# Left-over block before the last whole block, and one norm set for batches 2 and 3, in a cross-covariance attention and channel-mix kernel

## Chip, cores and metric

The kernel runs on one core of a Trainium2 chip. The metric is device time in microseconds (us); the time before is the median of 8 executions. A profile is of one execution. TensorE is PE in its rows (PEld are its weight loads), VectorE is DVE, ScalarE is ACT, GpSimd is POOL, and SyncE is SP.

## What is computed

There are four batches of N = 6208 tokens with C = 256 channels. Channel attention makes x, and a channel mix with a token shift makes the output:

```python
qn = q / (np.linalg.norm(q, axis=1, keepdims=True) + 1e-06)   # norms over the tokens
kn = k / (np.linalg.norm(k, axis=1, keepdims=True) + 1e-06)
a = softmax(kn.transpose(0, 2, 1) @ qn / tau)                 # 256 x 256 per batch
x = v @ a
xk = mu_k * x + (1 - mu_k) * x_prev                           # x_prev: one token earlier
xr = mu_r * x + (1 - mu_r) * x_prev
k = np.maximum(xk @ w_k, 0.0)                                 # 256 -> 1024
out = sigmoid(xr @ w_r) * (k * k @ w_v)                       # 1024 -> 256
```

tau is 1. Inputs and output are float32; the matmuls work on bfloat16.

## The kernel before

**Blocks.** Each batch's tokens are cut into 12 blocks of 512 and 64 left over. The left-over tokens of the four batches make one further block of 256 tokens, called "left". There are 49 blocks; "left" stands last (`blocks`, `LAST`). A block has subtiles of 128 tokens: four, and two in "left".

**One loop sets the order.** Nothing is scheduled by a tool: the loop over i (block) and j (eight steps), from line 606, records the instructions of every engine in the order in which that engine runs them. T = 8i + j counts the steps. In one pass i the work of several blocks is interleaved:
- `up(i+1, j)` (lines 334, 338): two matmuls of 512 columns into a bank kT_ps (three of them), then a relu on ACT into kr. `square(i+1, ..)` (line 345) squares a pair of these on DVE into kk. The four pairs are recorded at steps 2, 4 and 6 and at step 0 of the next pass: that last one is the last square.
- `gate_mm(i, s)` (line 355): the gate's matmuls into g_ps, and `gate_act` (line 390) a tanh on ACT into res.
- `down(i, j)` (line 384): kk times w_v into v_ps, three and five matmuls of 256 columns for each subtile. `finish` (line 397) multiplies on DVE by the gate and sends the block's 512 KB to memory from SP (line 400).
- `x_half(i+2, ..)` (lines 260, 262): x of a later block, two matmuls and a copy on ACT. `mix_delta` and `mix` (lines 302, 313, and 305, 318 for "left"): xk and xr on DVE. xk of block i+2 is made at steps 4 to 6 and is needed by `up(i+2, 0)` at the start of the next pass.

**The next batch's attention runs beside this.** The rows of q and k of batches 1 to 3 come in 13 groups for each batch: the 64 left-over rows first, then 12 groups of 512 rows (`GORD`). `unit(b, g, s)` takes 128 rows: two matmuls into s_ps (line 424) and one squaring on ACT (line 428) into sq. `due` spreads the units of a batch over 12 passes. sq tiles share a ring of eight buffers (`f4`) with res.

**Norms.** The squares have to be summed over all rows. `take_sum` adds sq tiles on DVE: a first add (line 456) makes acc, further adds (line 459) add to it, and a merge (line 463) makes a 128 x 512 tile t1; the left-over rows are only cast to it (line 465). `take_norm` multiplies t1 by a column of ones on PE: four matmuls of one column into n_ps (line 476), a norm set, copied by ACT (line 478) into a column of ssq. In batches 2 and 3 three groups share one acc (`MERGE = 3`), which gives five sets for a batch with that of the left-over rows; batch 1 has a set for each group. After a batch's last set comes its softmax chain (`softmax_pieces`): ten small pieces at ten steps, mostly on DVE.

**When a sum runs.** `sums` is a queue; `unit` appends to it, and the loop takes one entry at a step by

```python
            if j in (2, 3, 6, 7) or len(sums) > 2:
                take_sum()
```

**The end.** The last pass has only the down-projection of "left". `down` gives each of its two subtiles a bank of its own (line 370), multiplies it by the gate (line 373), and sends its rows in pieces of 64 KB, half on SP's queue and half on ACT's (line 378). The banks v_ps are two and go round.

Of the kernel before, what the change touches and what calls it, by code (L numbers as in the profile page):

```python
# [10 lines left out]
F32 = mybir.dt.float32  # L11
# [3 lines left out]
OP = mybir.AluOpType  # L15
# [3 lines left out]
def kernel(  # L19
# [13 lines left out]
    nc = tc.nc  # L33
    B, N, C = q.shape
    D = C
    DF = moe_w_k.shape[1]
    P = 128
    M = 512
    S = M // P
    assert C == 256 and DF == 1024  # L40
    NB = N // M
    L = N - NB * M
# [11 lines left out]
    ps = ctx.enter_context(tc.tile_pool(name="ps", bufs=1, space=bass.MemoryType.PSUM))  # L54
# [36 lines left out]
    NPE = 4  # L91
# [121 lines left out]
                pn.tile([P, 2], F32, name="sm"), pn.tile([P, 2], F32, name="mx"))  # L213


    blocks = [(b, t) for b in range(B) for t in range(NB)] + ["left"]
    NBLK = len(blocks)
    LAST = NBLK - 1
    LR = L + 16
    xl = const.tile([P, 2, B, L + 1], BF16, name="xl")  # L220
    st = {}

    def size(i):
        return M if i < LAST else B * L

    def v_load(i):
        b, t = blocks[i]
# [67 lines left out]
    def mix_delta(i):  # L295
        delta = p2.tile([P, 2, M], BF16, name="delta", tag="delta", bufs=2)
        st[i, "d"] = delta
        st[i, "xk"] = p2.tile([P, 2, M], BF16, name="xk", tag="xk", bufs=3)
        st[i, "xr"] = p2.tile([P, 2, M], BF16, name="xr", tag="xr", bufs=3)
        if i < LAST:  # L300
            o = blocks[i][1] * M
            nc.vector.tensor_tensor(delta, X[:, :, o + 1:o + 1 + M], X[:, :, o:o + M], op=OP.subtract)  # L302
        else:
            for dh in range(2):
                nc.vector.tensor_tensor(delta[:, dh, :B * L].rearrange("p (b l) -> p b l", b=B),
                                        xl[:, dh, :, 1:], xl[:, dh, :, :L], op=OP.subtract)

    def mix(i, key, dh):
        mu = mu_k_t if key == "xk" else mu_r_t
        o = st[i, key]  # L310
        if i < LAST:
            c = blocks[i][1] * M
            nc.vector.scalar_tensor_tensor(o[:, dh], st[i, "d"][:, dh], mu[:, dh:dh + 1],  # L313
                                           X[:, dh, c:c + M], op0=OP.mult, op1=OP.add)
        else:
            def r(a):
                return a.rearrange("p (b l) -> p b l", b=B)
            nc.vector.scalar_tensor_tensor(r(o[:, dh, :B * L]), r(st[i, "d"][:, dh, :B * L]), mu[:, dh:dh + 1],
                                           xl[:, dh, :, :L], op0=OP.mult, op1=OP.add)
# [27 lines left out]
    def gate_mm(i, s):  # L347
        if s * P >= size(i):
            return
        if s % 2 == 0:  # L350
            st[i, "g", s // 2] = ps.tile([P, 2, D], F32, name="g_ps", tag="g")
        g_ps = st[i, "g", s // 2]
        xr = st[i, "xr"]
        for dh in range(2):
            nc.tensor.matmul(g_ps[:, s % 2], xr[:, dh, s * P:(s + 1) * P], w_r_sb[:, dh, :],  # L355
                             start=s % 2 == 0 and dh == 0, stop=dh == 1, skip_group_check=True)

    def down(i, j):
        s, h = divmod(j, 2)
        if s * P >= size(i):  # L360
            return
        kk = st[i, "kk"]
        if (i, "res") not in st:
            st[i, "res"] = pq.tile([P, S, D], F32, name="res", tag="f4", bufs=NF)
        if i == LAST:
            if h == 0:
                st[i, "v1", s] = ps.tile([P, 2, D], F32, name="v_ps", tag="v", bufs=2)
            v_ps = st[i, "v1", s][:, 0]
            for fh in (range(3) if h == 0 else range(3, 8)):
                nc.tensor.matmul(v_ps, kk[:, fh, s * P:(s + 1) * P], w_v_sb[:, fh, :], start=fh == 0, stop=fh == 7)  # L370
            if h == 1:
                res = st[i, "res"]
                nc.vector.scalar_tensor_tensor(res[:, s], res[:, s], 1.0, v_ps, op0=OP.add, op1=OP.mult)  # L373
                for b in range(B):
                    u, o = divmod(b * L, P)
                    if u == s:
                        eng = nc.sync if o == 0 else nc.scalar
                        eng.dma_start(out[b, NB * M:, :], res[o:o + L, s, :])
            return
        if j % 4 == 0:  # L380
            st[i, "v", s // 2] = ps.tile([P, 2, D], F32, name="v_ps", tag="v", bufs=2)
        v_ps = st[i, "v", s // 2]
        for fh in (range(3) if h == 0 else range(3, 8)):
            nc.tensor.matmul(v_ps[:, s % 2], kk[:, fh, s * P:(s + 1) * P], w_v_sb[:, fh, :],  # L384
                             start=s % 2 == 0 and fh == 0, stop=fh == 7, skip_group_check=True)

    def gate_act(i, u):

        if (i, "g", u) in st:
            nc.scalar.activation(st[i, "res"][:, 2 * u:2 * u + 2], st.pop((i, "g", u)), AF.Tanh, scale=0.5)  # L390

    def finish(i, u):
        if (i, "v", u) not in st:
            return
        res = st[i, "res"]
        r = res[:, 2 * u:2 * u + 2]
        nc.vector.scalar_tensor_tensor(r, r, 1.0, st.pop((i, "v", u)), op0=OP.add, op1=OP.mult)  # L397
        if u == 1:
            b, t = blocks[i]
            nc.sync.dma_start(out[b, t * M:(t + 1) * M, :].rearrange("(s p) c -> p s c", p=P), res)  # L400

# [4 lines left out]
    sums = []  # L406
# [8 lines left out]
    def unit(b, g, s):  # L415
        rows, n = rows_of(g)
        if g == GORD[0] and s == 0:
            cov[b] = ps.tile([P, 2, C], F32, name="s_ps", tag="s")
            ssq[b] = pn.tile([P, 4, NB + 1], F32, name="ssq")
            ncol[b] = 0  # L420
        G = groups[b, g]
        qk = G["qk"]
        for ih in range(2):
            nc.tensor.matmul(cov[b][:, ih, :], qk[:rows, s, 1, ih * P:(ih + 1) * P], qk[:rows, s, 0, :],  # L424
                             start=g == GORD[0] and s == 0 and ih == 0, stop=g == GORD[-1], skip_group_check=True)
        if s % 2 == 0:
            G["sq", s // 2] = pq.tile([P, 2, 2, C], F32, name="sq", tag="f4", bufs=NF)
        nc.scalar.activation(G["sq", s // 2][:rows, s % 2], qk[:rows, s], AF.Square)  # L428
        if s == n - 1:
            if n == S:  # L430
                m = (GORD.index(g) - 1) % MERGE if b > 1 else 0
                if m == 0:
                    sums.append((b, g, 1))
                else:
                    sums.append((b, g, 3))
                    sums.append((b, g, 4))
                if b == 1 or m == MERGE - 1:
                    sums.append((b, g, 2))
            else:
                sums.append((b, g, 0))  # L440

    sums = []
    norms = []
    acc = {}

    MERGE = 3

    def take_sum():
        if not sums:
            return  # L450
        b, g, w = sums.pop(0)
        rows, n = rows_of(g)
        G = groups[b, g]
        if w == 1:
            acc[b] = pq.tile([P, 2, 2, C], F32, name="acc", tag="acc", bufs=2)
            nc.vector.tensor_tensor(acc[b], G["sq", 0], G["sq", 1], op=OP.add)
            return
        if w > 2:
            nc.vector.tensor_tensor(acc[b], acc[b], G["sq", w - 3], op=OP.add)  # L459
            return  # L460
        t1 = pq.tile([P, 2, C], BF16, name="t1", tag="t1", bufs=4)
        if w == 2:
            nc.vector.tensor_tensor(t1, acc[b][:, 0], acc[b][:, 1], op=OP.add)
        else:
            nc.vector.tensor_copy(t1[:rows], G["sq", 0][:rows, 0])
        norms.append((b, g, t1, T + 2))
# [139 lines left out]
    for i in range(-2, NBLK):  # L606
        for j in range(8):
            T = i * 8 + j
            if i == LAST - 1 and j == 7:

                st[LAST, "res"] = pq.tile([P, S, D], F32, name="res", tag="f4", bufs=NF)
                for s in range(2):
                    gate_mm(LAST, s)
                gate_act(LAST, 0)
            if j in (2, 6):
                gate_act(i, j // 4)
            if 0 <= i + 1 < NBLK:
                up(i + 1, j)
# [12 lines left out]
            n = i + 2  # L631
            if n == 0 and j == 0:
                x_first()
            if 0 < n < LAST:
                if j == 0:
                    x_half(n, 0)
                if j == 2:
                    x_half(n, 1)
# [10 lines left out]
                mix(i + 1, "xr", j)  # L649
            if j == 7 and 2 <= i + 3 < NPE:  # L650
                v_transpose_pe(i + 3, st.pop((i + 3, "v")), 0, S, "s")
            if j == 1 and NPE <= i + 5 < LAST:
                v_transpose_dma(i + 5)
            if j == 2 and NPE < i + 7 < LAST:
                v_load(i + 7)
            bank_x = i >= 0 and i % NB == 6 and j == 4
            if chain and (chain[0] is None or chain[0].__name__ != "bcast" or j in (4, 6)):
# [3 lines left out]
                    bank_x = f.__name__ == "bcast"  # L661
            if j in (4, 6) and not bank_x or j in (3, 5) and len(norms) > 1:
                take_norm()
            if j in (2, 3, 6, 7) or len(sums) > 2:
                take_sum()
            for u in due.get(T, []):
                b, g, s = units[u]
# [48 lines left out]
```

## Time and profile before

| | |
|---|---|
| median of 8 runs | 512.21 us (511.02 to 514.38) |
| the profiled execution | 513.14 us, of it the span 511.4 us |
| mean granted TensorE clock | 0.994 |
| last DVE instruction | starts at 506.96 us, takes 0.42 us |
| sums of batches 2 and 3 | about 140 to 370 us |

A row of the timeline has start, duration, engine, line, operation, output <- inputs, shape, and how many instructions it merges; in square brackets stands the idle time before it and what ended it. Durations of matmuls include the passage through the array, so that rows of back-to-back matmuls overlap: the distance of their starts is what one of them costs.

### The profile page before, as it was taken

The numbers are of one execution on the slowest core, as the hardware profiler recorded it, in microseconds if no ns is written. First come the engines' busy times: TensorE is split into PE (matmuls) and PEld (weight loads), VectorE is DVE, ScalarE is ACT, GpSimd is POOL, SyncE is SP. The second block draws the span as 40 slices with busy tenths as digits, with TensorE's granted clock in tenths as the row PEclk, the third lists the DMA queues.
The fourth block names the chain that finished last, engine by engine and source line by source line (L and its number), as shares of the span: only waits on it lengthen the run. The fifth ranks groups of instructions, "written<-read, shape, count | busy, mean of one in ns | idle before, by whom it ended". The sixth has DMA issues, their size and how long they took to land. (4 is left out here: it accounts for less than half of the span.)

```text
span 511.4 us, 9779 instructions
## 1 busy us (share of the span) xinstructions
PE 494.0 (97%) x3720; PEld 339.4 (66%) x3720; DVE 445.1 (87%) x704; ACT 432.4 (85%) x817; POOL 106.2 (21%) x145
## 2 busy tenths in 40 slices
PE   5799999999999999999999999999999999999996
PEld 2474677776676677677666767767666666666675
DVE  3467799999999999999999999999998787878884
ACT  6787999999999898898998899899787877787773
POOL 0036523422431231221342132100121100000000
PEclk9999999999999999999999999999999999999999
DMA  8999999999999999999699999952299674332213
GB/s 313 396 304 190 195 190 197 195 218 195 171 194 181 167 174 165 174 166 162 111 185 196 189 181 157 151 128 72 62 152 163 104 144 114 76 105 61 75 50 104
DMA packets 143343, 83.48 MB, mean 163 GB/s; under 512 B 51200, under 2 KB 139840, under 8 KB 143296
## 3 DMA queue, kind: packets, MB, share of 16 engines
q0 software_dynamic: 65808, 33.01, 52.4%
q1 hardware_dynamic: 77328, 49.72, 43.9%
q8 instruction: 29, 0.48, 0.4%
q10 hardware_dynamic: 160, 0.13, 0.1%
q14 instruction: 18, 0.15, 0.1%
HBM read 78.71 MB, written 25.43 MB: 204 GB/s over the span
## 5 line engine op out<-in xcount | busy, mean ns | idle before, releaser
L338 ACT ACTIVATE kr<-kT_ps 128x512 bf16<-128x512 f32 (+1 forms) x392 | 232.8, 597 | 36.7 <-PE kT_ps L334 28.7
L384 PE MATMUL v_ps<-w_v_sb,kk 128*128 128x256 bf16 x1536 | 230.5, 273 | 0.6 <-DMA w_v_sb<-in_moe_w_v_dram 0.6
L334 PE MATMUL kT_ps<-xk,w_k_sb 128*128 128x512 bf16 (+1 forms) x780 | 230.4, 377 | 0.5 <-DVE xk L313 0.5
L384 PEld LDWEIGHTS <-kk 128*128 128x128 bf16 x1536 | 150.2, 98 | 58.4 <-issue 0.8
L345 DVE TENSOR_TENSOR kk<-kr 128x1024 bf16<-128x1024 bf16 (+1 forms) x196 | 132.7, 681 | 34.9 <-ACT kr L338 34.2
L428 ACT ACTIVATE sq<-qk 128x512 f32<-128x512 bf16 (+1 forms) x147 | 93.3, 635 | 0.0
L334 PEld LDWEIGHTS <-w_k_sb 128*128 128x128 bf16 x780 | 74.8, 98 | 21.6 <-issue 0.9
L355 PE MATMUL g_ps<-w_r_sb,xr 128*128 128x256 bf16 x388 | 73.9, 273 | 0.0
L313 DVE SCALAR_TENSOR_TENSOR xr<-delta,mu_r_t,X 128x512 bf16<-128x512 bf16 x96 | 71.3, 744 | 0.0
L262 ACT CAST X<-xT_ps 128x512 bf16<-128x512 f32 x94 | 55.6, 591 | 18.5 <-PE xT_ps L260 17.9
L355 PEld LDWEIGHTS <-xr 128*128 128x128 bf16 x388 | 37.9, 98 | 45.5 <-issue 1.3
L313 DVE SCALAR_TENSOR_TENSOR xk<-delta,mu_k_t,X 128x512 bf16<-128x512 bf16 x96 | 67.6, 745 | 0.0
L397 DVE SCALAR_TENSOR_TENSOR res<-res,v_ps 128x512 f32<-128x512 f32 x96 | 65.2, 679 | 0.0
L413 POOL DMA_DIRECT2D qk<-in_q_dram x39 | 28.6, 733 | 148.0 <-ACT sq L428 121.2
L390 ACT ACTIVATE res<-g_ps 128x512 f32<-128x512 f32 x97 | 57.9, 597 | 0.4 <-PE g_ps L355 0.4
L260 PE MATMUL xT_ps<-vT,a_sb 128*128 128x512 bf16 x188 | 55.9, 379 | 0.2 <-ACT vT L253 0.2
L424 PE MATMUL s_ps<-qk 128*128 128x256 bf16 (+1 forms) x294 | 56.1, 272 | 0.0
L229 POOL DMA_DIRECT2D v_bf<-in_v_dram x48 | 36.7, 768 | 63.3 <-DMA vT<-v_bf 49.3
L459 DVE TENSOR_TENSOR acc<-acc,sq 128x1024 f32<-128x1024 f32 x32 | 39.0, 1220 | 1.0
L424 PEld LDWEIGHTS <-qk 128*128 128x128 bf16 (+1 forms) x294 | 27.5, 98 | 12.3 <-issue 1.3
L302 DVE TENSOR_TENSOR delta<-X 128x1024 bf16<-128x1024 bf16 x48 | 32.9, 686 | 0.6 <-ACT X L272 0.3
L413 POOL DMA_DIRECT2D qk<-in_k_dram x39 | 28.8, 737 | 10.7 <-DMA qk<-in_k_dram 5.2
(75 smaller groups left out, 243.9 us busy)
## 6 DMA issues: line engine op xcount, KB each, us to landing
out_dram<-res SPq DMA_DIRECT2D x48, 512.0 KB, 4.0
v_bf<-in_v_dram POOLq DMA_DIRECT2D x48, 256.0 KB, 10.0
qk<-in_q_dram POOLq DMA_DIRECT2D x36, 256.0 KB, 10.8
qk<-in_k_dram POOLq DMA_DIRECT2D x36, 256.0 KB, 11.2
f<-in_q_dram SPq DMA_DIRECT2D x12, 512.0 KB, 8.1
f<-in_k_dram SPq DMA_DIRECT2D x10, 512.0 KB, 9.4
f<-in_k_dram SPq DMA_DIRECT2D x3, 256.0 KB, 6.7
vT<-v_bf SPq DMA_TRANSPOSE x44, 7.8
```

The source lines that it names most:

```text
L260: nc.tensor.matmul(xT_ps, a_sb[:, b, ih, dh * P:(dh + 1) * P], vT[:, :, ih, :], start=ih == 0, stop=ih == 1)
L313: nc.vector.scalar_tensor_tensor(o[:, dh], st[i, "d"][:, dh], mu[:, dh:dh + 1], X[:, dh, c:c + M], op0=OP.mult, op1=OP.add)
L334: nc.tensor.matmul(kT_ps[:, :m], w_k_sb[:, dh, fh * P:(fh + 1) * P], xk[:, dh, :m], start=dh == 0, stop=dh == 1)
L338: nc.scalar.activation(st[i, "kr", fh // 2][:, fh % 2, :m], kT_ps[:, :m], AF.Relu, scale=RH)
L345: nc.vector.tensor_tensor(st[i, "kk"][:, fh - 1:fh + 1, :m], kr[:, :, :m], kr[:, :, :m], op=OP.mult)
L355: nc.tensor.matmul(g_ps[:, s % 2], xr[:, dh, s * P:(s + 1) * P], w_r_sb[:, dh, :], start=s % 2 == 0 and dh == 0, stop=dh == 1, skip_group_ ...
L384: nc.tensor.matmul(v_ps[:, s % 2], kk[:, fh, s * P:(s + 1) * P], w_v_sb[:, fh, :], start=s % 2 == 0 and fh == 0, stop=fh == 7, skip_group_ ...
L390: nc.scalar.activation(st[i, "res"][:, 2 * u:2 * u + 2], st.pop((i, "g", u)), AF.Tanh, scale=0.5)
L397: nc.vector.scalar_tensor_tensor(r, r, 1.0, st.pop((i, "v", u)), op0=OP.add, op1=OP.mult)
L413: nc.gpsimd.dma_start(qk[:rows, :n, i], src_rows(t, b, g))
L424: nc.tensor.matmul(cov[b][:, ih, :], qk[:rows, s, 1, ih * P:(ih + 1) * P], qk[:rows, s, 0, :], start=g == GORD[0] and s == 0 and ih == 0, ...
L428: nc.scalar.activation(G["sq", s // 2][:rows, s % 2], qk[:rows, s], AF.Square)
```

## The change

"left" moves one place ahead of the last whole block, and the last pass handles that whole block: its gates are all computed at the pass's start, the second pair of them in the bank of s_ps, and its down-projection runs by a table `LASTD` of (subtile, first, end) at given steps: first the first four of eight partial products of subtiles 0 to 2, then their rest, then subtile 3. Each subtile has a bank of its own, is multiplied on its own, and is sent on its own; the last one in two halves, on SP's and ACT's queue. In batches 2 and 3 all groups share one acc: the left-over rows' sq is added to it (entry 5), and there is one merge and one norm set for a batch. Away from batch 1 and from a batch's last three groups, a sum runs only at steps 3 and 7, or when more than four wait. The program has 32 matmuls and 32 weight loads fewer; all of these are n_ps.

```diff
-    blocks = [(b, t) for b in range(B) for t in range(NB)] + ["left"]
+    blocks = [(b, t) for b in range(B) for t in range(NB)]
+    blocks.insert(-1, "left")
...
+    LEFT = LAST - 1
+    LASTD = {0: [(0, 0, 4), (1, 0, 4), (2, 0, 4)], 2: [(0, 4, 8)], 3: [(1, 4, 8)], 4: [(2, 4, 8)], 6: [(3, 0, 8)]}
...
-            st[i, "g", s // 2] = ps.tile([P, 2, D], F32, name="g_ps", tag="g")
+            st[i, "g", s // 2] = ps.tile([P, 2, D], F32, name="g_ps", tag="s" if i == LAST and s else "g")
...
+            for s, f0, f1 in LASTD.get(j, ()):
+                if f0 == 0:
+                    tag, bufs = (("v", 2), ("v", 2), ("xT", 1), ("kT", 3))[s]
+                    st[i, "v1", s] = ps.tile([P, 2, D], F32, name="v_ps", tag=tag, bufs=bufs)
+                v_ps = st[i, "v1", s][:, 0]
+                for fh in range(f0, f1):
+                    nc.tensor.matmul(v_ps, kk[:, fh, s * P:(s + 1) * P], w_v_sb[:, fh, :],
+                                     start=fh == 0, stop=fh == 7)
+                if f1 == 8:
+                    res = st[i, "res"]
+                    nc.vector.scalar_tensor_tensor(res[:, s], res[:, s], 1.0, v_ps, op0=OP.add, op1=OP.mult)
+                    b, t = blocks[i]
+                    n = P if s < S - 1 else P // 2
+                    for u in range(P // n):
+                        o = t * M + s * P + u * n
+                        (nc.scalar if u else nc.sync).dma_start(out[b, o:o + n, :], res[u * n:(u + 1) * n, s, :])
...
-        if u == 1:
+        if i == LEFT:
+            for b in range(B):
+                s, o = divmod(b * L, P)
+                nc.sync.dma_start(out[b, NB * M:, :], res[o:o + L, s, :])
+        elif u == 1:
...
-                m = (GORD.index(g) - 1) % MERGE if b > 1 else 0
+                m = GORD.index(g) - 1 if b > 1 else 0
                 if m == 0:
                     sums.append((b, g, 1))
+                    if b > 1:
+                        sums.append((b, GORD[0], 5))
...
-                if b == 1 or m == MERGE - 1:
+                if b == 1 or g == GORD[-1]:
                     sums.append((b, g, 2))
-            else:
+            elif b == 1:
                 sums.append((b, g, 0))
...
+        if w == 5:
+            nc.vector.tensor_tensor(acc[b][:rows, 0], acc[b][:rows, 0], G["sq", 0][:rows, 0], op=OP.add)
+            return
...
-            if i == LAST - 1 and j == 7:
+            if i == LAST and j == 0:
...
-                for s in range(2):
+                for s in range(4):
                     gate_mm(LAST, s)
-                gate_act(LAST, 0)
-            if j in (2, 6):
+                for u in range(2):
+                    gate_act(LAST, u)
+            if j in (2, 6) and i != LAST:
...
-            if j in (2, 3, 6, 7) or len(sums) > 2:
+            near = sums and (sums[0][0] == 1 or sums[0][1] in GORD[-3:])
+            if j in (2, 3, 6, 7) and near or j in (3,7) or len(sums) > (2 if near else 4):
                 take_sum()
```

More of the change, by code (lines that the diff above doesn't have):

```diff
@@ L223, in size @@
     def size(i):
-        return M if i < LAST else B * L
+        return M if i != LEFT else B * L
     def v_load(i):
@@ L299, in mix_delta @@
         st[i, "xr"] = p2.tile([P, 2, M], BF16, name="xr", tag="xr", bufs=3)
-        if i < LAST:
+        if i != LEFT:
             o = blocks[i][1] * M
@@ L310, in mix @@
         o = st[i, key]
-        if i < LAST:
+        if i != LEFT:
             c = blocks[i][1] * M
@@ L365, in down @@
         if i == LAST:
[L366 to L378, printed above, removed]
+            for s, f0, f1 in LASTD.get(j, ()):
[14 more added lines that the diff above has]
+                        (nc.scalar if u else nc.sync).dma_start(out[b, o:o + n, :], res[u * n:(u + 1) * n, s, :])
             return
@@ L444 @@
     acc = {}
-    MERGE = 3
     def take_sum():
@@ L633 @@
                 x_first()
-            if 0 < n < LAST:
+            if 0 < n < NBLK and n != LEFT:
                 if j == 0:
@@ L651 @@
                 v_transpose_pe(i + 3, st.pop((i + 3, "v")), 0, S, "s")
-            if j == 1 and NPE <= i + 5 < LAST:
+            if j == 1 and NPE <= i + 5 < NBLK and i + 5 != LEFT:
                 v_transpose_dma(i + 5)
-            if j == 2 and NPE < i + 7 < LAST:
+            if j == 2 and NPE < i + 7 < NBLK and i + 7 != LEFT:
                 v_load(i + 7)
```

## Prediction

> **What bounds the kernel now.** First the page's engine row: TensorE is busy almost throughout, VectorE not far behind.
>
> ```profile
> PE 494.0 (97%) x3720; PEld 339.4 (66%) x3720; DVE 445.1 (87%) x704; ACT 432.4 (85%) x817; POOL 106.2 (21%) x145
> ```
>
> Ends of matmuls are modelled, so a busy PE may hide waits. I therefore read starts: in the stream a matmul of 512 columns starts 0.216 us after the one before, one of 256 columns 0.109 us, from 66 us to 505 us almost without exception. TensorE's queue is the clock of the kernel there; another engine counts only where it makes a matmul late. The table by stretches (columns: PE, PEld, DVE, ACT, POOL, granted clock, DMA) says how near the others are where the sums of batches 2 and 3 lie (about 140 to 370 us):
>
> ```profile
> 140.00:255.00 115.00, 115.00 (x842) 80.05 (x840) 110.95 (x164) 104.06 (x203) 28.91 (x39) 1.00 1.20 167
> 255.00:370.00 115.00, 114.50 (x833) 79.18 (x831) 110.85 (x167) 102.39 (x200) 22.16 (x30) 1.00 0.92 148
> ```
>
> VectorE works 96% of this stretch: it is what can make PE wait. Third, the waits of PE from 100 us to the end hold only two causes: kT_ps for xk (0.5 us in two places), and at the end v_ps for res. The chain that ended last says no more than that the end is PE, then DVE, then the transfer. So time can come from three things: matmuls that vanish, the few late ones, and what follows the last.
>
> **1. Norm sets.** A set is four matmuls of one column on four weight loads. In time on PE, from the timeline of PE:
>
> ```profile
> 171.25 0.24 PE L476 MATMUL n_ps<-ones_b,t 128*128 128x1 bf16 x4
> 171.36 0.59 PE L334 MATMUL kT_ps<-xk,w_k_sb 128*128 128x512 bf16 x2
> ```
>
> The stream goes on 0.11 us after the set began. The left-over rows' own set costs more, since it has 64 rows:
>
> ```profile
> 260.40 0.49 PE L384 MATMUL v_ps<-w_v_sb,kk 128*128 128x256 bf16 x3
> 260.82 0.25 PE L476 MATMUL n_ps<-ones_b,t 64*128 64x1 bf16 x4
> 261.00 0.60 PE L334 MATMUL kT_ps<-xk,w_k_sb 128*128 128x512 bf16 x2
> ```
>
> Three v_ps of 0.109 us take PE to 260.73; the next real matmul starts at 261.00: 0.27 us. Each of batches 2 and 3 has five sets now (left-over, then one for three groups) and keeps one. Gone per batch: 0.27 + 3 x 0.11 = 0.60 us; **1.2 us** for two. A rule of the Trainium skill ("TensorE: Matmul & The Clock Gate", section "LDWEIGHTS (loading the stationary operand)") gives a weight load its columns / 1.2 ns, 107 ns for 128, and the profile does list about 97 ns for each. If these tiny matmuls went at the pace of their loads, a set would be 0.43 us and 8 sets 3.4 us. The starts contradict that: 0.11 us for four pairs. I take the starts.
>
> **2. VectorE's sums.** Per batch now: 4 first adds and 16 adds of 1.22, 4 merges of 0.69, a cast of 0.41: 27.6 us. Then: 23 adds of 1.22, one merge, and one add of the left-over's 64 rows x 512, which no row shows: between that cast's 0.41 and the 128 x 512 float rows' 0.68; I take 0.6. Sum 29.4: 1.7 us more per batch. ScalarE loses four copies of 0.17 us. DVE's 110.9 of 115 us becomes 112.6 of 114.4: still under PE, if spread well. So placing decides. A block of two adds now, from DVE's timeline:
>
> ```profile
> 294.10 0.69 DVE L345 TENSOR_TENSOR kk<-kr 128x1024 bf16<-128x1024 bf16 x1
> 294.70 2.55 DVE L459 TENSOR_TENSOR acc<-acc,sq 128x1024 f32<-128x1024 f32 x2
> 297.17 0.69 DVE L345 TENSOR_TENSOR kk<-kr 128x1024 bf16<-128x1024 bf16 x1
> ...
> 298.97 1.41 DVE L313 SCALAR_TENSOR_TENSOR xk<-delta,mu_k_t,X 128x512 bf16<-128x512 bf16 x2
> 300.30 1.38 DVE L345 TENSOR_TENSOR kk<-kr 128x1024 bf16<-128x1024 bf16 x2
> ```
>
> Both adds stand ahead of xk (steps 2 and 3); xk ends at 300.38, and the matmul that needs it starts at 301.14. The last square (second of the two at 300.30) ends at 301.68, and the first matmul that reads its columns starts at 303.31: 1.6 us of cover. After the change one add stands at step 3 and one at step 7, between the last two squares. Then the square of 297.17 starts when its kr is ready (ACT ends it at 296.66), all behind comes 0.5 us earlier, the second add takes about 300.4 to 301.7, and the last square ends near 302.4: cover 1.0 us instead of 1.6. Queued behind the moved add are that square, xr and the finish of the block before. The lag is worked off in the next block, where DVE again waits for kr (0.2 us by this sum). I book **nothing** lost; were the cover gone, about 22 blocks would each pay the excess.
>
> What that does to PE's late matmuls:
>
> ```profile
> 271.76 0.38 PE L334 MATMUL kT_ps<-xk,w_k_sb 128*128 128x512 bf16 x1
> 272.37 0.38 PE L334 MATMUL kT_ps<-xk,w_k_sb 128*128 128x512 bf16 x1 [0.23 <-DVE xk L313]
> ```
>
> 0.61 between starts instead of 0.22: 0.39 us lost, in the block after batch 2's softmax chain. Ahead of this xk stand now cast, first add and two adds; then first add, small add, one add: 0.41 + 1.22 - 0.6 = 1.0 less, so it is in time. The same at 155.38 (0.14). A third, 0.45 at 367.63, stays: the three sums before batch 3's chain keep their steps, and the blocks ahead (29 and 30) now have two adds each, so DVE arrives up to 0.2 later: 0.15 worse. At the two healed places the last square is now the tight one (0.2 us of cover by the same sum; PE may lose up to 0.3). Net gain 0.53 - 0.15 = **0.35 us**, ends 0 and 0.9.
>
> **3. The end.** The order of matmuls changes, their number not. PE and then DVE:
>
> ```profile
> 504.47 1.22 PE L370 MATMUL v_ps<-w_v_sb,kk 128*128 128x256 bf16 x8
> 505.89 1.03 PE L370 MATMUL v_ps<-w_v_sb,kk 128*128 128x256 bf16 x8 [0.20 <-DVE res L397]
> ```
>
> ```profile
> 505.15 0.68 DVE L397 SCALAR_TENSOR_TENSOR res<-res,v_ps 128x512 f32<-128x512 f32 x1
> 505.75 0.42 DVE L373 SCALAR_TENSOR_TENSOR res<-res,v_ps 128x256 f32<-128x256 f32 x1
> 506.96 0.42 DVE L373 SCALAR_TENSOR_TENSOR res<-res,v_ps 128x256 f32<-128x256 f32 x1 [0.79 <-PE v_ps L370]
> ```
>
> The 16 matmuls should start within 15 x 0.109 = 1.64 us of 504.47; the last starts at 506.65, 2.18 later: 0.54 lost, first for the square of the last pair, then for a bank that the finish at 505.15 frees. After the change, from the start of the left-over's down-projection block: 16 ups of 0.216 and 20 of 0.109 take 5.6 us, 8 gate matmuls 0.9, twelve of down on pairs 0 and 1, 1.3; so the last pair is wanted at about 8.0. ScalarE paces the ups there (0.60 against 0.43), its last relu ends near 6.8, the square near 7.6. No wait, 0.4 us of cover; each part of the product has its own bank (v, v, xT, kT). One new wait: the block before has only 256-column ups and lasts 7.0 us, and DVE, from the relu at 4.3 through square (0.42), delta, finish (0.68 each) and two xk (1.41), less 0.08 overlap each, ends near 7.3 where PE wants xk at 7.24: 0.1 us (0 to 0.4). Gain **0.45 us** (0.1 to 0.54).
>
> Then the transfer. The last pieces are 64 KB on SP's and ScalarE's queue in both. Now:
>
> ```profile
> DMA to landing us min/median/max: 2.4/2.9/3.3
> ```
>
> That is the four left-over pieces (line 378), the last issued at 507.41, beside the 512 KB of the last whole block, issued at 505.86. After, the whole block ahead sends its 512 KB some eight microseconds before the last pieces, and SP issues the left-over's four pieces (about 0.5 us each) before the last block's first: they are out by then. The last two pieces follow three of 128 KB that start 2.3 us ahead. The nearest row without traffic is the first load of 64 KB at 2.1 us: **0.3 us** less than 2.4; ends 0, and 0.5 (512 KB at its quickest is 2.9, some 1.3 of it moving at the page's best 396 GB/s; 1.6 + 0.3 = 1.9). Against the change speaks the Trainium skill ("DMA: Bandwidth & Descriptors", section "Measured (HBM→SBUF, 128 partitions, SWDGE, issued from GpSimd)"): batch to 1 MiB, since 64 KB takes 0.95 us of engine time. Five pieces one after another would be 4.75 us and land about 0.6 later than now, an end 0.9 worse than I book. But here 768 KB in five transfers, issued within 1.6 us, were all down 2.4 us after the last issue; I take the row.
>
> **Sum.** 1.2 + 0.35 + 0.45 + 0.3 = 2.3 us. The profiled execution took 513.14 us (span 511.4, 1.7 around it) and should take 510.8. It lies 0.9 above the median of the runs shown, 512.21; the difference carries over: **509.9 us**.
>
> **Rivals.** *Only the norm sets count* (0.20): the end's waits move instead of going, since bare ups run at ScalarE's pace and the short block makes xk late; the pieces land as now; the last squares take back the two healed places. 1.2 - 0.3 = 0.9 us: 511.3, not to be told from no change (0.3%, 1.5 us, is about what a measurement of this kernel can tell). For it: both new covers are under half a microsecond. Against: each is positive by rows. *VectorE becomes the bound* (0.06), on the other side: the add at step 7 makes the last square late in every block of batches 2 and 3. It decides once DVE enters that step over 1.0 us behind; at 0.2 us of wait a block, 22 blocks lose 4.4, so 512.21 + 4.4 - 2.3 = 514.3. For it: 96% busy. Against: DVE stood waiting for kr in 14 squares of 95 there. *More goes* (0.12): the wait at 367.63 too, the whole 0.54 and 0.5 of the transfer: 1.2 + 0.98 + 0.54 + 0.5 = 3.2, 509.0. My forecast has 0.62, with 509.2 to 510.6 as its own range. Faster by over 0.3%: 0.74, within: 0.20, slower: 0.06. Range 508.8 to 511.4, from the bounds summed to the case of the norm sets alone.
>
> **What would show it.** n_ps x60 instead of x92; no jump of starts near 155 and 272; adds of 1.22 at regular distances of half a block, DVE near 98% from 140 to 370 us; at the end 32 v_ps without a gap and the last pieces landing in about 2.1 us. Wrong if PE shows waits for kk in most blocks between 140 and 370 us, or a gap over 0.5 us in the last two blocks.

## Result, and the profile after

The changed kernel takes **509.38 us** (median of 20 runs, 508.4 to 513.06); the kernel before, run beside it, 511.36 (57 runs). The ratio is 0.9963 [0.995, 0.9976]: about 1.9 us less, between 1.2 and 2.6. Two further measurements of the same program, on two different chips, gave 0.9934 [0.9906, 0.9962] and 0.9956 [0.9943, 0.9969], that is 3.4 and 2.3 us less; the three intervals overlap.

The profiled execution took 509.67 us, its span is 507.9 us, its granted clock 0.998. The engine row of the page:

```profile
PE 491.7 (97%) x3688; PEld 338.4 (67%) x3688; DVE 447.2 (88%) x705; ACT 430.6 (85%) x809; POOL 104.7 (21%) x145
```

PE and ACT have less to do, DVE more. The group of n_ps has 60 matmuls instead of 92, and in the last column four of 64 rows instead of twelve:

```profile
L493 PE MATMUL n_ps<-ones_b,t x60: 160/163/174, 57.5 to 363.6; 128*128 128x1 bf16 x56, 64*128 64x1 bf16 x4
```

The whole span is a poor measure of so small a change. The first n_ps set starts between 56.6 and 60.6 us in the profiles of these kernels, which all do the same up to there (but for e5's padding), so several tenths or whole microseconds of a single span belong to the head. I therefore cut each trace into pieces: from the first matmul of n_ps to the last, from there to the start of the last matmul, and from that matmul's end to the end of the span. That end is modelled, but it lies 0.27 us after the start in every profile, so it adds nothing to a difference. Some profiles lack matmul records (e9 lists 3625 of 3688); the distance between two starts doesn't depend on them.

| us | first to last n_ps | last n_ps to last matmul's start | last matmul's end to span's end |
|---|---|---|---|
| before | 307.41 | 140.06 | 4.45 |
| after | 306.05 | 139.58 | 4.47 |
| gain | 1.36 | 0.47 | -0.02 |

The remaining 1.66 us of the difference in span (511.4 to 507.9) lie ahead of the first n_ps, where both kernels do the same, and aren't the change's.

DVE's share after, in the two stretches of the sums (columns: PE, PEld, DVE, ACT, POOL, clock, DMA share and rate), and the new group of the small add:

```profile
138.00:253.00 115.00, 114.98 (x828) 79.89 (x827) 112.50 (x168) 104.02 (x201) 28.97 (x39) 1.00 1.28 166
253.00:368.00 115.00, 114.72 (x824) 79.51 (x822) 112.50 (x167) 102.74 (x198) 22.01 (x30) 1.00 0.97 148
```

```profile
L473 DVE TENSOR_TENSOR acc<-acc,sq 64x512 f32<-64x512 f32 x2 | 1.3, 673 | 0.0
```

Before, DVE has 110.85 in both of these stretches. 112.50 of 115 us are 97.8%; 112.6 and "near 98%" were forecast. The small add takes 0.67 us, booked at 0.6. In PE's timeline after, the place of the wait at 271.76 has none: two kT_ps and then the next matmul, 0.43 us later.

```profile
269.05 0.38 PE L438 MATMUL s_ps<-qk 128*128 128x256 bf16 x2
269.27 0.59 PE L339 MATMUL kT_ps<-xk,w_k_sb 128*128 128x512 bf16 x2
269.70 0.38 PE L360 MATMUL g_ps<-w_r_sb,xr 128*128 128x256 bf16 x2
```

The end, in PE's timeline after:

```profile
493.19 0.66 PE L339 MATMUL kT_ps<-xk,w_k_sb 128*128 128x512 bf16 x2
...
498.90 1.04 PE L360 MATMUL g_ps<-w_r_sb,xr 128*128 128x256 bf16 x8
499.77 3.66 PE L379 MATMUL v_ps<-w_v_sb,kk 128*128 128x256 bf16 x32
```

Eight gate matmuls and 32 v_ps run in a row: 499.77 is 8 x 0.109 after 498.90, and the one row of 32 has no wait in it. The last square starts on DVE at 499.90 and takes 0.69 us; the first v_ps that reads its columns is the fifteenth, near 501.30.

### The profile page after: what moved, and what is told of

Same layout as the page of the kernel before. It is cut to its first block, busy times and chain, and to the rows that moved or that the text cites. A ratio compares the mean times of both kernels' runs of the same rounds, so it can differ in the third digit from the quotient of the medians.

```text
span 507.9 us, 9714 instructions
## 1 busy us (share of the span) xinstructions
PE 491.7 (97%) x3688; PEld 338.4 (67%) x3688; DVE 447.2 (88%) x705; ACT 430.6 (85%) x809; POOL 104.7 (21%) x145
## 4 chain that ended last, share of the span: by engine, by line
PE 83%; DMA 7%; DVE 6%; ACT 2%; issue 1%; SPq 1%; POOL 0%; ACTq 0%
PE v_ps L394 30%; PE kT_ps L339 30%; PE g_ps L360 8%; PE xT_ps L265 7%; PE s_ps L438 6%; DMA f<-in_q_dram 4%; DMA f<-in_k_dram 2%; DMA v_bf<-in_v_dram 2%; DVE kk L350 1%; DVE acc L476 1%; DVE xk L318 1%; DVE res L407 1%; DVE xr L318 1%; PE v_ps L379 1%; ACT kr L343 1%
## 5 line engine op out<-in xcount | busy, mean ns | idle before, releaser
L394 PE MATMUL v_ps<-w_v_sb,kk 128*128 128x256 bf16 x1520 | 228.0, 273 | 0.0
L394 PEld LDWEIGHTS <-kk 128*128 128x128 bf16 x1520 | 148.6, 98 | 57.1
L476 DVE TENSOR_TENSOR acc<-acc,sq 128x1024 f32<-128x1024 f32 x44 | 53.6, 1218 | 0.1
```

## Experiments

**The two halves alone.** The theory: the norm sets and the placing of the sums give about 1.35 us ahead of the last set, the order of the blocks about 0.5 us on PE and up to 0.7 behind the last matmul. The rivals of the prediction: only the norm sets count, or VectorE gives part of it back in every block. (The letters in the recorded expectations are those of each expectation alone.) `e1_order_only` is the change with the norm sets and sum steps of before:

```diff
-                m = GORD.index(g) - 1 if b > 1 else 0
+                m = (GORD.index(g) - 1) % MERGE if b > 1 else 0
...
-                    if b > 1:
-                        sums.append((b, GORD[0], 5))
...
-                if b == 1 or g == GORD[-1]:
+                if b == 1 or m == MERGE - 1:
...
-            elif b == 1:
+            else:
...
-            near = sums and (sums[0][0] == 1 or sums[0][1] in GORD[-3:])
-            if j in (2, 3, 6, 7) and near or j in (3,7) or len(sums) > (2 if near else 4):
+            if j in (2, 3, 6, 7) or len(sums) > 2:
```

> The new order of blocks and the new end alone; norm sets and sums as before. Theory A (the change's gain has three parts: 1.2 us of norm sets, 0.2 us net of late matmuls, 0.5 us at the end; a further gain of the last transfer is undone by a 16 KB instruction packet that sits on one of the 16 DMA engines while the last pieces move, because PE's program is 64 instructions shorter): n_ps x92, from the first to the last n_ps set 307.4 us as before, from the last set to the last matmul's start about 139.6 us (140.1 before), and as PE's program is as long as before, no packet at the end: last matmul's end to the span's end about 3.8 us instead of 4.45. Time 0.5 + 0.6 = 1.1 us under before, ratio about 0.998. Rival B (the last pieces take 2.5 to 2.9 us whatever else moves): the end after the last matmul stays 4.45 us, ratio 0.999. Rival C (the whole gain is the end's): ratio 0.996, as with the whole change.

Measured: 510.44 us, 0.9974 [0.9962, 0.9987]. Pieces 307.43, 139.59, 3.75: the first is that of before, the second that of the change, and the end is 0.70 shorter. `e2_norms_only` is the kernel before with these lines the other way round and the code of the small add, entry 5, so "left" stands last.

> One norm set for batches 2 and 3 and the new steps of the sums alone; the left-over block stays last. Theory A: n_ps x60, first to last n_ps set 306.0 us (307.4 before), last set to last matmul's start 140.1 us as before, ratio about 0.997 if no packet meets the last pieces, 0.998 if one does. Rival C (the gain is the end's): ratio 1.000. If the rule of 107 ns for a weight load priced a set (0.43 us), first to last set would be 303.9 us or less and the ratio 0.993.

Measured: 510.06 us, 0.9972 [0.9958, 0.9986]. Pieces 306.07, 140.06, 4.46: the first is that of the change, both others are those of before. The waits at the end are there as before; for v_ps in the last subtile:

```profile
502.01 1.03 PE L370 MATMUL v_ps<-w_v_sb,kk 128*128 128x256 bf16 x8 [0.20 <-DVE res L397]
```

So the halves add up, piece by piece, and each is worth something: that only the norm sets count is refuted by e1, and that the whole gain is the end's by e2. A price of 107 ns for each load would have made the first piece 3.4 us shorter, 304.0; it is 1.34 shorter.

**Is it the fewer sets, or the steps?** `e3_old_steps` keeps the single set and lets the sums run at the old steps:

```diff
-            near = sums and (sums[0][0] == 1 or sums[0][1] in GORD[-3:])
-            if j in (2, 3, 6, 7) and near or j in (3,7) or len(sums) > (2 if near else 4):
+            if j in (2, 3, 6, 7) or len(sums) > 2:
```

> The change with the sums at the old steps (2, 3, 6, 7, or when more than two wait); the merging into one set stays. It tells what the new steps are worth. Theory A (adds ahead of xk make it late only where the chain's pieces or a third add come on top): no waits at 230 and 346 us, but in the second block after each batch's end the xk is late by more than before, 0.3 to 0.6 us instead of 0.14 and 0.39, since the left-over rows' small add stands there too; first to last n_ps set 306.4 to 306.7 us instead of 306.05. Rival (the even steps are what keeps VectorE from becoming the bound): waits in most blocks, first to last set over 309 us, slower than before.

Measured: 512.49 us, 0.9996 [0.997, 1.0022]. Pieces 307.90, 139.58, 4.38. The first is 1.85 us longer than the change's, three to five times what I expected, and 0.5 longer than that of the kernel before: in these traces, the merging with the old steps is a loss. The times don't separate e3 from the kernel before.

Its waits lie near 155 and 272 us, the blocks after the two earlier softmax chains, with one more at 266 and one at the end of batch 3; at each of the two, two follow each other:

```profile
155.26 0.38 PE L438 MATMUL s_ps<-qk 128*128 128x256 bf16 x2
155.89 0.39 PE L339 MATMUL kT_ps<-xk,w_k_sb 128*128 128x512 bf16 x1 [0.25 <-ACT kr L343]
156.55 0.38 PE L339 MATMUL kT_ps<-xk,w_k_sb 128*128 128x512 bf16 x1 [0.27 <-DVE xk L318]
```

Two s_ps cost 0.22, so the first kT_ps is 0.41 late, and the next, 0.66 after it instead of 0.22, loses 0.44. Most blocks have no wait even with 98% of DVE in use and two adds ahead of xk. So there is no price in every block; at the old steps DVE's lateness costs where the chain's pieces come on top.

**Can the new waits be taken away?** The changed kernel has two waits that the kernel before had not, at 229.88 and 345.72 us (0.18 and 0.17). `e4_even_sums` spreads the sums still further: each is queued half a group earlier, and only the last group keeps the old steps.

```diff
+        if b > 1 and n == S and s == 1 and g > 0:
+            sums.append((b, g, 3))
...
-                    sums.append((b, g, 3))
...
-            near = sums and (sums[0][0] == 1 or sums[0][1] in GORD[-3:])
-            if j in (2, 3, 6, 7) and near or j in (3,7) or len(sums) > (2 if near else 4):
+            near = sums and (sums[0][0] == 1 or sums[0][1] == GORD[-1])
+            if j in (2, 3, 6, 7) and near or j in (3,7) or len(sums) > (2 if near else 4) or sums and sums[0][2] == 5:
```

> The change, with the adds of batches 2 and 3 evened out: an add is queued as soon as its sq tile is whole, only the last group counts as near, and the left-over rows' small add is taken at once, so that each block has one add ahead of xk and one behind it, and only one add and the merge stand ahead of xk at the end of batch 3 instead of two adds and the merge. Theory A (the late matmuls at 230, 346 and 365 us, 0.18 + 0.17 + 0.45 us, come from adds ahead of xk): all three vanish or shrink under 0.1, first to last n_ps set 305.6 us instead of 306.0, last set to last matmul's start 139.2 instead of 139.6; 0.7 us faster than the change, ratio about 0.995. Rival D (they come from the softmax chain's or the units' instructions, not from the adds): they stay, ratio 0.996.

Measured: 510.35 us, 0.9974 [0.9963, 0.9985]. Pieces 307.56, 139.35, 3.75: the first is 1.5 us longer than the change's. A miss. The two waits did go, and the one at batch 3's end fell from 0.44 to 0.25. But the adds came half a block earlier into the blocks that hold the softmax chain of the batch before, and made new waits there: 0.42, 0.31 and 0.18 near 145, 153 and 156 us, and the same three again from 262 to 272. The first of them:

```profile
145.19 0.49 PE L394 MATMUL v_ps<-w_v_sb,kk 128*128 128x256 bf16 x3
145.94 0.28 PE L394 MATMUL v_ps<-w_v_sb,kk 128*128 128x256 bf16 x1 [0.26 <-DVE kk L350]
```

This is the wait for the last square that I had feared for every block; it comes only here.

`e10_two_sets` takes the other way: acc is restarted at the tenth group. In each batch that saves DVE an add of 1.22 us, and costs it a merge of 0.69 and PE a norm set.

```diff
+    CUT = 9
...
-                m = GORD.index(g) - 1 if b > 1 else 0
+                m = (GORD.index(g) - 1) % CUT if b > 1 else 0
...
-                    if b > 1:
+                    if b > 1 and g == 0:
...
-                if b == 1 or g == GORD[-1]:
+                if b == 1 or m == CUT - 1 or g == GORD[-1]:
```

> The change, with two norm sets for each of batches 2 and 3 instead of one: acc is started anew at the tenth group, so that one first add of 1.22 us and a merge of 0.69 stand in the place of two adds there, 0.5 us less on DVE, for 0.10 us more on PE. Theory A (the late matmuls at 230, 346 and 365 us are DVE's work piling up ahead of xk; the trace shows DVE without a gap from 345 to 367 us): the first two vanish, the third falls from 0.45 to under 0.2; first to last n_ps set 306.05 + 0.21 - 0.36 = 305.9 us, last set to last matmul's start 139.2 to 139.3 instead of 139.58; 0.5 us under the change. Rival (one set is best since each set costs PE): 0.2 us over the change.

Measured: 509.15 us, 0.996 [0.9947, 0.9972]. The pieces are 306.08, 139.90, 3.74: the first two together are 0.34 longer than the change's. A miss too: the waits at 230 and 346 went (0.35), but the two sets cost 0.21, and one wait of 0.36 us came at 367, ahead of the old one, and one of 0.16 at 274. What the saved add became is in DVE's timeline:

```profile
343.50 0.68 DVE L481 TENSOR_TENSOR t<-acc 128x512 bf16<-128x512 f32 x1
345.06 0.69 DVE L350 TENSOR_TENSOR kk<-kr 128x1024 bf16<-128x1024 bf16 x1 [0.88 <-ACT kr L343]
```

DVE, ahead of its work, idled 0.88 us for ACT's kr. From there to about 369 us it has no gap, so it meets the chain of batch 3 as late as it can be; a wait that PE is spared at 346 only lets PE arrive earlier at 367.

**The end.** Three kernels each undo one detail of the last block. `e6_one_dma` sends it as one transfer of 512 KB:

```diff
-                    b, t = blocks[i]
-                    n = P if s < S - 1 else P // 2
-                    for u in range(P // n):
-                        o = t * M + s * P + u * n
-                        (nc.scalar if u else nc.sync).dma_start(out[b, o:o + n, :], res[u * n:(u + 1) * n, s, :])
+                    if s == S - 1:
+                        b, t = blocks[i]
+                        nc.sync.dma_start(out[b, t * M:(t + 1) * M, :].rearrange("(s p) c -> p s c", p=P), res)
```

> The change, with the last block sent as one transfer of 512 KB on SP's queue after its last multiply, instead of five pieces. By the rule that transfers should be batched, it would be no slower. Theory A (only what is left to move after the last multiply counts): 512 KB took 2.9 us at its quickest and 4.0 in the median, against about 2.2 for the last piece without a packet in the way: the last matmul's end to the span's end grows from 3.75 (4.47 in the change's first profile) to 4.6 to 5.5 us; time 0.5 to 1.5 us over the change, ratio 0.997 to 0.999.

Measured: 510.92 us, 0.9959 [0.9943, 0.9975] (the change beside it: 510.25, 0.9934), which times alone don't separate. Pieces 306.05, 139.58, 4.66: the trace shows an end 0.9 us longer than the 3.73 and 3.76 of the change's two undisturbed profiles (below); 0.75 of it, against e9, is the landing. The transfer, from issue to landing:

```profile
DMA to landing us min/median/max: 2.9/2.9/2.9
```

`e7_gate_bank` puts both gate pairs into one bank g, so that the second pair waits until ACT has read the first:

```diff
-            st[i, "g", s // 2] = ps.tile([P, 2, D], F32, name="g_ps", tag="s" if i == LAST and s else "g")
+            st[i, "g", s // 2] = ps.tile([P, 2, D], F32, name="g_ps", tag="g")
...
-                for s in range(4):
-                    gate_mm(LAST, s)
                 for u in range(2):
+                    gate_mm(LAST, 2 * u)
+                    gate_mm(LAST, 2 * u + 1)
                     gate_act(LAST, u)
```

> The change, with both pairs of the last block's gates in the one bank g_ps (the tanh of the first pair is recorded between them); the subtiles keep their own banks. Theory A: the second pair waits for the first tanh, which stands behind the last relu on ScalarE: it ended at 500.3 us in the change's profile, where the second pair could start at 499.3: a gap of 1.0 us on PE before the second pair, last set to last matmul's start 140.5 us instead of 139.6. Rival (the bank is free in time, or the matmuls that follow were waiting for squares anyhow, so the gap is filled): under 139.8 us.

Measured: 511.13 us, 0.9977 [0.9958, 0.9997]. Pieces 306.05, 140.66, 3.74; all of the 1.08 us is one gap:

```profile
500.69 0.60 PE L360 MATMUL g_ps<-w_r_sb,xr 128*128 128x256 bf16 x4
502.20 0.60 PE L360 MATMUL g_ps<-w_r_sb,xr 128*128 128x256 bf16 x4 [0.91 <-ACT res L400]
```

`e8_v_banks` gives the four subtiles the two v banks in turn, which delays subtile 2 to step 4:

```diff
-    LASTD = {0: [(0, 0, 4), (1, 0, 4), (2, 0, 4)], 2: [(0, 4, 8)], 3: [(1, 4, 8)], 4: [(2, 4, 8)], 6: [(3, 0, 8)]}
+    LASTD = {0: [(0, 0, 4), (1, 0, 4)], 2: [(0, 4, 8)], 3: [(1, 4, 8)], 4: [(2, 0, 8)], 6: [(3, 0, 8)]}
...
-                    tag, bufs = (("v", 2), ("v", 2), ("xT", 1), ("kT", 3))[s]
+                    tag, bufs = ("v", 2)
```

> The change, with the last block's four subtiles in the two banks v_ps in turn, and subtile 2's first half moved behind subtile 1's second (gates keep their two banks). Theory A: subtile 2 needs the bank that subtile 0's multiply frees, which DVE ends 0.4 to 0.7 us after subtile 0's last matmul, while subtile 1's second half takes 0.44: PE waits 0.0 to 0.3 us there; the last pair's square is wanted 0.44 us earlier, which its cover of 0.4 just about holds; last set to last matmul's start 139.6 to 140.0 us instead of 139.58. So the subtiles' own banks are worth little beside the gates' own (1.08 us). Rival (the change of banks in the product is what removed the waits of 0.17 and 0.37 us at the end): over 140.0 us.

Measured: 509.58 us, 0.996 [0.9946, 0.9974]. Pieces 306.06, 139.88, 3.74: 0.30 us lost in one gap inside the 32 v_ps, too little for the times. Their row takes 3.95 us instead of 3.66:

```profile
500.41 3.95 PE L379 MATMUL v_ps<-w_v_sb,kk 128*128 128x256 bf16 x32
```

**Why did the first profile show no shorter transfer?** It ends 4.47 us after the last matmul, e1 3.75. In its DMA view, from 504.2 us to the end, there is a packet of another kind beside the last pieces:

```profile
q1 hardware_dynamic: 184, 0.16, 12.8%
q10 hardware_dynamic: 80, 0.07, 6.2%
q8 instruction: 1, 0.02, 1.4%
...
out_dram<-res SPq DMA_DIRECT2D x1, 64.0 KB, 2.8
out_dram<-res ACTq DMA_DIRECT2D x1, 64.0 KB, 2.9
```

The packet, of 16 KB, came at 504.59 and took 0.96 us. Each piece lands in 16 parts. Of the last two pieces, 15 parts had landed by 505.84 and 506.13, the last ones only at 506.71 and 506.86. That these are the parts behind the packet, on one DMA engine, is inferred from this. My first idea was that the packet's moment follows from the length of PE's program, which the change shortens by 64 instructions. `e5_pad32` lengthens it again by 32 one-column matmuls in the head, whose results nobody reads:

```diff
+    PAD = 32
...
+        if n == FQ and src == 0:
+            for u in range(PAD):
+                nc.tensor.matmul(f_ps[:, :1], ident, ident[:, :1], start=True, stop=True)
```

> The change, with 32 matmuls of one column (and their weight loads) added in the first microseconds, where PE waits for data anyway; their results are not used. PE's program is then as long as before, and what it fetches falls at other times. Theory A (instruction packet): the packet leaves the end, the last pieces land about 2.2 us after their issue instead of 2.9, last matmul's end to the span's end 3.7 to 3.8 us instead of 4.47, 0.7 us faster than the change, ratio 0.995. Rival B (the last pieces take that long by themselves): the end stays 4.4 to 4.5 us, ratio 0.996.

Measured: 509.08 us, 0.9957 [0.9941, 0.9972]. Pieces 306.06, 139.59, 3.73; the packet at 495.70, out of the way. That fits the idea, but it doesn't carry it: e4 has no padding and ends in 3.75, and the changed program itself, run twice more as `e9_after_again` and `e11_after_third`, decides it.

> The changed kernel again, for a second profile of the very same program. Theory A as it stands after the first four runs (order alone and the padded version ended 3.75 and 3.73 us after the last matmul; so did the version with evened sums, whose PE program is as short as the change's, with its instruction packet 1.7 us ahead of the last matmul): the packet among the last pieces is chance, not tied to the program's length; this profile then ends about 3.75 us after the last matmul, with all else as in the first: first to last n_ps set 306.05 us, last set to last matmul's start 139.6 us, late matmuls of 0.18, 0.17 and 0.45 us. If the packet belongs to this program, the end is 4.4 to 4.5 us again.

> The changed kernel beside these two on the same chip. First to last n_ps set 306.05 us, last set to last matmul's start 139.58; after the last matmul 3.75 us, or 4.4 to 4.5 if an instruction packet meets the last pieces. Theory A of the version with two sets has it 0.5 us slower than that version.

Measured: 510.25 us, 0.9934 [0.9906, 0.9962], pieces 306.05, 139.58, 3.73; and 508.97 us, 0.9956 [0.9943, 0.9969], pieces 306.05, 139.59, 3.76. The packet comes in each, but at 510.26 in the one, after its end at 509.0, and at 502.89 in the other, before the last pieces are issued; e9's last pieces, from 504 us to the end:

```profile
out_dram<-res SPq DMA_DIRECT2D x3, 128.0 KB, 1.8
out_dram<-res SPq DMA_DIRECT2D x1, 64.0 KB, 1.9
out_dram<-res ACTq DMA_DIRECT2D x1, 64.0 KB, 2.2
```

The same program has it or not: the idea of the length falls. Of the ten profiles with the five pieces, the end is free of it in eight (3.73 to 3.76); in two (the first, and e3 with 4.38) it isn't. What sets its moment stays open.

**What the 0.7 us consist of.** Not all of it is the transfer. From the last matmul's end to the last landing it is 3.10 us before and 2.70 in e9: 0.40 less. The rest of the span, behind that landing, fell from 1.35 to 1.04 us. SyncE closes each of these kernels with nine waits, about 0.06 us apart if nothing holds them, and two more after that. SyncE's waits behind the last landing, before and in e9:

```profile
L711 SPq EVENT_SEMAPHORE  x10: 17/28/28, 510.0 to 511.3; - x10
L731 SPq EVENT_SEMAPHORE  x5: 17/28/28, 508.0 to 509.0; - x5
```

Before, eight of the nine come after the last landing, in e9 three: five times 0.06 is the 0.31. All ten profiles with the five pieces have three, e2 has eight as before, and e6 six.

No experiment made a version that beats the change by more than the noise: e5 and e10 have medians of 509.08 and 509.15, the change 508.97 on the chip of the latter.

## Why the forecast held, step by step

| step | forecast, us | measured, us |
|---|---|---|
| 1. eight norm sets | 1.2 | 1.17 |
| 2. late matmuls | 0.35 (0 to 0.9) | 0.18 |
| 3. the end on PE | 0.45 | 0.47 |
| 3. the last transfer | 0.3 (0 to 0.5) | 0.40; 0.34 lost in the first profile |
| SyncE's closing waits | not in the forecast | 0.31 |
| sum | 2.3 | 2.5; 1.8 in the first profile; 1.9 (1.2 to 2.6) by the runs |

The gain is what was forecast. The time of 509.9 was met to 0.5 us partly by luck: the kernel before came out at 511.36 instead of 512.21, 0.85 lower, and the medians differ by 2.0 us instead of 2.3. The low end of the range, 508.8, is also 0.2 below what the stated bounds add up to (509.0). Neither changes the outcome.

**Norm sets: right.** By starts, a set of 128 rows costs 0.104 us and the set of 64 rows 0.278: 2 x (0.278 + 3 x 0.104) = 1.17. With the late matmuls' 0.18 that makes 1.35 of the 1.36 us of the first piece, and e2's 1.34 agrees; the price by loads does not.

**Late matmuls: right in where they go, wrong in what comes.** The waits at 155 and 272 us (0.14 and 0.39) are gone, as forecast. The one at 367 was forecast to grow by 0.15 because the blocks ahead hold more adds; it stayed at 0.44 (at 364.62 after). What I did not see are the waits at 229.88 and 345.72, 0.35 together. PE and, ahead of it, DVE at the first of them:

```profile
228.90 0.59 PE L339 MATMUL kT_ps<-xk,w_k_sb 128*128 128x512 bf16 x2
229.33 0.71 PE L394 MATMUL v_ps<-w_v_sb,kk 128*128 128x256 bf16 x5
229.88 0.77 PE L339 MATMUL kT_ps<-xk,w_k_sb 128*128 128x512 bf16 x2
230.49 0.38 PE L360 MATMUL g_ps<-w_r_sb,xr 128*128 128x256 bf16 x2
```

```profile
219.09 0.75 DVE L318 SCALAR_TENSOR_TENSOR xk<-delta,mu_k_t,X 128x512 bf16<-128x512 bf16 x1
...
220.35 1.22 DVE L476 TENSOR_TENSOR acc<-acc,sq 128x1024 f32<-128x1024 f32 x1
...
224.61 2.48 DVE L476 TENSOR_TENSOR acc<-acc,sq 128x1024 f32<-128x1024 f32 x2
...
228.81 1.41 DVE L318 SCALAR_TENSOR_TENSOR xk<-delta,mu_k_t,X 128x512 bf16<-128x512 bf16 x2
```

Two kT_ps after 229.88 take 0.61 instead of 0.43. Between the two xk lie three adds, 3.7 us, where a block otherwise has two: the last three groups of a batch go back to the old steps, so the block in which this begins has an add at step 7 from the new rule, and two at steps 2 and 3 of the next pass from the old. The step that failed is "The three sums before batch 3's chain keep their steps": I priced the blocks on either side of that border and not the border. The net was half of what I booked, inside the ends given.

**VectorE's cover: right.** The forecast put the last square's cover at 1.0 us in a steady block; it is 0.76 to 1.06. Over each such block PE waits for nothing. At the two healed places it was forecast at 0.2, and is 0.29 and 0.22 (near 156 and 272 us), which still sufficed. e4 shows the cover gone, at up to 0.42 us the time. "Booked nothing" holds only with the adds as the change places them; by e3 the placing is worth 1.85 us, more than all the norm sets, and this the prediction did not price.

**The end on PE: right.** The two stalls of 0.17 and 0.37 are gone; the new wait of the first up of the last block for xk, forecast at 0.1, is 0.07 (493.19). The last pair's square has 0.7 us of cover, not 0.4: it starts at 499.90, right after its relu, and is done at 500.59.

**The transfer: right mechanism, and a term left out.** The forecast went from 2.4 to 2.1 us for the last piece. 2.4 is the quickest of the four pieces, not the one that ends the kernel: all were down 2.61 us after the last issue, on ScalarE's queue. In e9 that last piece takes 2.16, near the 2.1 that was booked. It is issued 0.04 later after the last matmul, so 0.40 us are left, within the ends. What the forecast lacked is SyncE's closing waits, 0.31. The first profile showed none of the gain in its end (-0.02): there the landing was 0.34 later than before, through the packet above. The Trainium skill's rule of batching ("DMA: Bandwidth & Descriptors", section "Measured (HBM→SBUF, 128 partitions, SWDGE, issued from GpSimd)"), from loads, spoke against the five pieces with 0.9 us. It did not hold for this store: e6, with a single transfer, lands 0.75 us later. What counts at the end is what remains to be sent after the last multiply, 128 KB against 512.

**Chances.** The mechanism is the one forecast. *Only the norm sets count* needed the end's waits to move and the pieces to land as before; e1 shows 0.47 gained on PE and 0.40 in the landing. *VectorE becomes the bound* needed a wait in most blocks; there are two small ones in two batches.

## What to carry to other kernels

- Price tiny matmuls by the distance of starts in the trace, not by the length of their rows or loads; and where an engine that is 96% busy gets more work, the price of that work is decided by where in the block it stands: the same adds cost 1.85 us more at the old steps than at the new.
- Where a rule for placing work changes along a queue, look at the block in which one rule ends and the next begins: both rules' work meets there. And where an engine has no gap between two waits, a wait removed at the first comes back at the second.
- What follows the last multiply is a path of its own: split the last output so that little of it is left then (0.75 us here), and give the gates and the parts banks of their own (1.08 and 0.30 us). Look also behind the last landing: how many closing waits are still ahead there was worth 0.31 us.

## Not expected of the hardware

- A packet of 16 KB in a queue named "instruction" took 0.96 us beside the last pieces, and the last landing came 0.74 us later than without it (3.44 and 2.70 us after the last matmul's end). The Trainium skill ("Runtime: NRT & Kernel Launch", section "Instruction fetch mechanics") says that each engine's instructions are refilled in blocks of 16 KiB by a DMA queue and calls the cost mostly hidden. The size agrees; at the kernel's end the cost was not hidden.
- Norm sets of 64 rows among matmuls of 128 rows cost 0.278 us instead of 0.104. Most of the difference stands at the switch to 64 rows and back: 0.096 and 0.068 us. The s_ps matmuls of the left-over rows, also 64 rows among 128, have 0.095 and 0.094 there (at 243.8 us after). No run changed the rows alone, so that the switch is their cause is argued and not shown.
- At the end of e9 the stores of 128 KB landed 1.7 to 1.8 us after their issue, sooner than the last two of 64 KB (1.9 and 2.2) and than the 64 KB load (2.1) that I had taken as the quickest row.

Left open: the wait of 0.44 us at batch 3's end, which no version here took away (e4 left 0.25 of it), and what sets the moment of the instruction packet.
